# Attention and two MoE layers on one core: the first stretch's order rewritten by tile size of the matmuls, the last 64 keys of PV padded to 128 rows, and each buffer's turn stated

## Chip, core and metric

One core of a Trainium2 chip runs the whole program in one launch. The metric is device time in microseconds from the launch to its end, the median of the timed runs; lower is better. Engines are named as in the profile: PE (TensorE), DVE (VectorE), ACT (ScalarE), POOL (GpSimd), SP (SyncE, whose one queue issues every DMA here).

## What is computed

Attention with a memory term, a dense layer with gated product, and a layer of four experts, all in float32 (weights of the dense layer arrive as 64-bit floats). B=2, H=8, S=576, D=64; 1152 tokens of 512.

```python
scores = q @ k.T / sqrt(D)                      # causal mask, softmax
local = softmax(scores) @ v                     # "PV"
q_p = where(q > 0, q, exp(q) - 1) + 1           # phi
mem_out = (q_p @ M_prev) / (q_p @ z_prev + 1e-6)
x = g * mem_out + (1 - g) * local               # g = sigmoid(beta), per head
h = ((x @ w1) * (x @ w2)) @ w3; y = h @ w_out
out = sum_e p[:, e] * (relu(y @ e_w1[e]) @ e_w2[e])
```

## The kernel before

The program has three stretches. The first (to about 207 us) computes attention for eight pairs of heads, and on the way converts the dense layer's weights from 64-bit patterns, forms W = w3 @ w_out, and does the gated product of batch 0. The second does batch 0's product with W and batch 1's gated product; the third is the four experts. Only the first is touched.

The first stretch's work is cut into parts of a few instructions, each a Python function under a short name, and `FIRST` (line 20) is a hand-stated list of these names: the parts are recorded in its order, and each engine, and SP's DMA queue, runs its own instructions in that order. An instruction waits until its inputs are there and its output buffer is free, and everything behind it on its engine waits with it.

A query row of 576 is four blocks of 128 (each head apart) and 64 more rows, which the two heads of a pair share as halves of one tile. For pair p the parts are:

- `@qp`, `@kp`, `@Vp`: loads of q, k, and both heads' v (SP).
- `sp0` to `sp3`: scores (PE; L253, tile 64x128, for query blocks 0 and 1, then 2, then 3; L242, 128x128, for the last 64 rows). `mpk`: mask and row minimum (DVE, L269). `xpk`: exponential (ACT, L274).
- `tpg`: transposes of the probabilities in seven groups (PE, L307); `cpg`: their copy to SBUF (ACT, L311). Group 6 is the last 64 keys of the last query block: 64 columns are transposed, giving a 64x128 tile.
- `vp0`, `vp1`: PV of each head (PE, L330), the output in halves of 64 columns, tile 128x64. `vp2`: PV of the last 64 rows (L340), four key blocks of 128 rows in tile 128x64 and the last of 64 rows in tile 64x64.
- `ep`, `fp`: phi (ACT, DVE). `np`: memory term (PE, L364 at 128x128, and for the last 64 rows two matmuls into column halves, L368, 128x64: a "column-half tail").
- `gp`, `jp`: normalising of memory term and PV out of PSUM (DVE, L350 to L356). `jap`: their sum (POOL). `zp`: transposes of the result (PE, L391) with their own column-half tail (L396). `zhp`, `zlp`: split of the result (ACT, DVE).

The dense layer's parts are `@o`, `@w`, `@b` (loads), `oa`/`od`/`oh`/`ol`, `wa`/`wd`/`wp`, `ba`/`bd`/`bp` (conversion: two ACT operations, two DVE operations L136 and L137, and splits), `w`u`_`k (PE, L473), `b`u`_`a (PE, L537), `y` (sums), `bs` (stores).

PSUM tiles of scores, memory term, PV and result share two buffers (tag S), transposes two (tag T), and the staged weights, converted floats and split weights have two or three each; a pool hands them out in turn. A staged weight load waits until its buffer's last user is done. float32 matmuls that are not in the r form run in two passes, so the profile counts two PE records for one such instruction of the program.

Of the kernel before, what the change touches and what calls it, by code (L numbers as in the profile page):

```python
# [19 lines left out]
@q0 @k0 @k1 @q1 e0 @V0 f0 s00 s01 @w0 m00 e1 m01 s02 x00 @V1 f1 s03 @o0 x01 m02 wa0 t00 @k2 t02 m03 @q2 s10 x02 wd0  # L20
@o1 s11 c00 wp0 c02 t01 m10 @o2 x03 t04 c01 s12 @w1 c04 m11 x10 t03 m12 v00 @mz c03 x11 t05 @bt v01 c05 x12 t06 t10
s13 c06 c10 e2 v02 m13 @q3 oa0 t14 gates j0 @k3 t13 c14 n0 @V2 x13 od0 t11 t12 s20 g0 c11 @o3 c12 oa1 m20 v10 ja0 c13
x20 t16 v11 f2 oh0 od1 t15 e3 s21 c15 ol0 @w2 c16 oa2 v12 m21 w0_0 oh1 j1 @V3 x21 s22 od2 s23 m22 t20 wa1 @w3 t22 m23
c20 n1 @k4 x22 wd1 @q4 s30 c22 g1 wp1 @w4 x23 t24 oh2 t21 m30 z0 c24 c21 ja1 t23 zh0 v20 c23 zl0 x30 f3 v21 oa3 ol1
# [24 lines left out]
""".split()
RING = 12  # L50
# [7 lines left out]
def kernel(  # L58
# [63 lines left out]
    def from64_acts(raw, tmp, nm):  # L122


        hi = raw[..., 1]
        shape = list(hi.shape)
        t = tmp.tile(shape, F32, tag="t64f", name=f"tf_{nm}", bufs=3)
# [58 lines left out]
    warm = psT.tile([P, 512], F32, tag="T", name="warm")  # L186
# [39 lines left out]
    def stage_a(p):  # L226
# [4 lines left out]
        def scores(*qb):  # L231
# [5 lines left out]
            ps = psS.tile([P, 2, 512], F32, tag="S", name=f"sc{qb[0]}_{p}")  # L237
# [22 lines left out]
        def peaks(qb, low=True, ex=True):  # L260
            for src, i, x in banks[qb]:
                w = src.shape[-1]
                if "mn" not in Pt:
                    Pt["mn"] = A2.tile([P, NS2 + 1], F32, tag="mn", name=f"mn{p}")
                one = Pt["mn"][:, 2 * i + x : 2 * i + x + 1]
                if (i, x) not in Pt:
                    Pt[i, x] = A2.tile([P, w], F32, tag=f"P{i}", name=f"P{i}_{2 * p + x}", bufs=3 if i < NB else 2)
# [25 lines left out]
    def stage_b(p):  # L293
# [5 lines left out]
        def trans(g):  # L299
            mine = GROUPS[g]  # L300
            kr = SB if mine[0][2] == NB else P

            def f():
                st[g] = ps = psT.tile([P, 512], F32, tag="T", name=f"pt{g}_{p}")[0:kr, 0 : P * len(mine)]
                for y, (i, x, j) in enumerate(mine):
                    k0 = j * P if i < NB else 0 if j == NB else SB + j * P
                    nc.tensor.transpose(ps[:, y * P : (y + 1) * P], prob_t[p][i, x][:, k0 : k0 + kr], identF)  # L307

            def copy():
                t = A1.tile([kr, P * len(mine)], F32, tag=f"pt{g}", name=f"pT{g}_{p}")  # L310
                nc.scalar.copy(t, st.pop(g))  # L311
                for y, n in enumerate(mine):
                    pt[n] = t[:, y * P : (y + 1) * P]

            parts.update({f"t{p}{g}": f, f"c{p}{g}": copy})

        def slots(nm):
            ps = psS.tile([P, 2, 512], F32, tag="S", name=f"{nm}{p}")
# [64 lines left out]
        def fin():  # L383
# [3 lines left out]
            st["x"] = ps = psS.tile([P, 1024], F32, tag="S", name=f"x{p}")[:, 0:S]  # L387
# [13 lines left out]
        def fin_lo():  # L401
# [4 lines left out]
            f"n{p}": mem, f"g{p}": mem_out, f"v{p}0": pv(0), f"v{p}1": pv(1), f"v{p}2": pv_last, f"j{p}": join,  # L406
            f"ja{p}": join_mem, f"z{p}": fin, f"zh{p}": fin_hi, f"zl{p}": fin_lo,
# [11 lines left out]
    def staging(nm):  # L419

        stage_n[0] += 1
        if stage_n[0] > RING:
            return pf.tile([P, 4, P, 2], U32, tag="raw", name=nm)
# [28 lines left out]
    def w_conv(u):  # L452
# [8 lines left out]
        def split():  # L461
            w3s[u] = pf.tile([P, 2, 4, P], F32R, tag="ws", name=f"w3s{u}")
# [38 lines left out]
    class BUnits:  # L501
# [23 lines left out]
        def conv(self, u):  # L525
            f = self.raw.pop(u)
            self.ws[u] = ws = self.pool.tile([P, 2, KD, P], F32R, tag="ws", name=f"ws{self.b}_{u}")
# [310 lines left out]
    def b1_prods(m):  # L838
# [20 lines left out]
        def keep(i):  # L859
            def f():  # L860
                if i == 0:
                    st["u"] = pf.tile([P, 3, HS], F32, tag="ws", name=f"u{m}")
# [301 lines left out]
```

## Time and profile before

| | |
|---|---|
| median of 3 timed runs | 687.31 us (687.28 to 687.6) |
| span of the profiled execution, first to last instruction | 685.4 us |
| what the median has beyond that span | 1.9 us |
| PE, DVE, ACT, POOL busy in the span | 99%, 65%, 56%, 54% |

The profile times each instruction of each engine. A PE record's end is modelled, and matmuls overlap, so the cost of a block of matmuls is read from its start to the start of what follows it. The two numbers ahead of a PE form, as in 128*64, are the rows and columns of the array that it uses, the tile size.

### The profile page before, as it was taken

The page shows a single profiled execution, that of the slowest core. Times are in us where ns is not written, and L with a number is a line of the kernel's source. Part 1 is how long each engine was busy: PE and PEld are TensorE (multiplying, and loading weights), DVE is VectorE, ACT ScalarE, POOL GpSimd, SP SyncE. Part 2 cuts the span into 40 slices and gives each one's busy share as a digit, 9 for nine tenths or more (in the row PEclk, how much of TensorE's full clock was granted, in tenths as well). Part 3 has the DMA queues.
Part 4 walks back from the last instruction along what each step waited for, and adds up shares of the span by engine and source line. Part 5 has one row for each costly group of instructions (what it writes and reads, how often), then busy time and mean ns, then how long its engine had stood idle before and what let it go on. Part 6 is the DMA issues. An engine that isn't in the chain of part 4 may idle for free.

```text
span 685.4 us, 12814 instructions
## 1 busy us (share of the span) xinstructions
PE 675.7 (99%) x4877; PEld 605.1 (88%) x4877; DVE 447.5 (65%) x839; ACT 382.5 (56%) x808; POOL 368.6 (54%) x366
## 2 busy tenths in 40 slices
PE   8999999999999999999999999999999999999997
PEld 5778799888999999998989998889999899989896
DVE  6689788998858499458575644356553556543563
ACT  6897787576744366454545554455544455553541
POOL 2034645565542111617777765677766678656660
PEclk9999999999999999999999999999999999999999
DMA  9556266633631212113213231323231132313401
GB/s 286 176 169 219 71 198 192 174 109 124 185 139 34 90 62 94 55 35 98 62 62 123 77 109 62 112 73 107 79 121 64 62 124 64 122 61 109 154 32 62
DMA packets 43405, 74.53 MB, mean 109 GB/s; under 512 B 14416, under 2 KB 14416, under 8 KB 43344
## 3 DMA queue, kind: packets, MB, share of 16 engines
q1 hardware_dynamic: 43344, 73.72, 33.9%
q8 instruction: 38, 0.62, 0.4%
q14 instruction: 23, 0.19, 0.1%
HBM read 67.15 MB, written 6.55 MB: 108 GB/s over the span
## 4 chain that ended last, share of the span: by engine, by line
PE 88%; DVE 6%; ACT 3%; issue 1%; DMA 1%; SPq 0%; DVEq 0%; ACTq 0%
PE o L990 28%; PE Z L1037 14%; PE c L587 7%; PE Q L1037 7%; PE wacc L473 7%; PE ab L537 5%; PE Zb L853 4%; PE R L1037 3%; PE a L330 2%; PE pt L307 2%; PE Qb L853 2%; PE sc L253 2%; ACT P L274 1%; DVE P L269 1%; PE Rb L853 1%
## 5 line engine op out<-in xcount | busy, mean ns | idle before, releaser
L990 PE MATMUL o<-w,he 128*128 128x512 f32 x864 | 224.8, 393 | 0.0
L104 POOL TENSOR_TENSOR w<-r,w 128x512 fp32r<-128x512 f32 x96 | 130.6, 1361 | 120.3 <-ACT w L728 120.2
L990 PEld LDWEIGHTS o<-w,he 128*128 128x128 f32 x864 | 153.8, 188 | 24.1
L975 ACT ACTIVATE he<-t 128x320 fp32r<-128x320 f32 (+1 forms) x96 | 42.7, 445 | 120.6 <-DVE t L1066 73.3
L976 DVE SCALAR_TENSOR_TENSOR he<-t,he 128x320 fp32r<-128x320 f32 (+1 forms) x96 | 57.4, 598 | 49.1 <-ACT he L975 49.1
L1059 DVE TENSOR_TENSOR t<-u,Q 128x320 f32<-128x320 f32 (+1 forms) x32 | 14.6, 455 | 83.2 <-ACT u L1057 83.2
L107 DVE TENSOR_TENSOR w<-r,w 128x512 fp32r<-128x512 f32 x64 | 66.2, 1036 | 0.0
L728 ACT CAST w<-r 128x512 fp32r<-128x512 f32 x96 | 58.9, 614 | 0.0
L537 PE MATMUL ab<-xT,ws 128*128 128x288 f32 x384 | 55.4, 299 | 1.2 <-ACT asb L547 0.7
L537 PEld LDWEIGHTS ab<-xT,ws 128*128 128x128 f32 x384 | 51.5, 188 | 3.1 <-issue 1.3
L587 PE MATMUL c<-hT,W 128*128 128x288 f32 (+2 forms) x384 | 52.6, 295 | 0.0
L587 PEld LDWEIGHTS c<-hT,W 128*128 128x128 f32 x384 | 51.6, 188 | 0.0
L1037 PE MATMUL Z<-X0T,w 128*128 128x320 f32 x288 | 50.2, 310 | 0.2 <-ACT s L1047 0.2
L1037 PEld LDWEIGHTS Z<-X0T,w 128*128 128x128 f32 x288 | 46.0, 188 | 4.4 <-ACT s L1047 0.6
L473 PE MATMUL wacc<-wo,w3s 128*128 128x512 f32 x192 | 48.2, 400 | 0.0
L1037 PEld LDWEIGHTS Z<-X1T,w 128*128 128x128 f32 x288 | 40.8, 189 | 4.1
L473 PEld LDWEIGHTS wacc<-wo,w3s 128*128 128x128 f32 x192 | 35.0, 188 | 8.8 <-issue 1.0
L1037 PE MATMUL Z<-X1T,w 128*128 128x256 f32 x288 | 42.1, 282 | 0.0
L269 DVE CUSTOM_DVE_ANT_0 P<-sc,mask 128x128 f32<-128x128 f32 (+4 forms) x72 | 33.7, 516 | 11.4 <-PE sc L253 6.4
L758 ACT CAST w<-r 128x512 fp32r<-128x512 f32 x64 | 39.5, 619 | 0.0
L274 ACT ACTIVATE P<-P,mn 128x128 f32<-128x128 f32 (+4 forms) x72 | 37.7, 582 | 1.0 <-DVE mn L269 0.9
L101 POOL TENSOR_SCALAR w3s<-tf_l 128x512 fp32r<-128x512 f32 x16 | 12.8, 799 | 43.9 <-DVE tf_l L137 33.3
(170 smaller groups left out, 1322.1 us busy)
## 6 DMA issues: line engine op xcount, KB each, us to landing
r<-in_moe_w_dram SPq DMA_DIRECT2D x64, 256.0 KB, 3.0
r<-in_moe_w_tiles_dram SPq DMA_DIRECT2D x64, 256.0 KB, 3.7
w3r<-in_moe_w_tiles_dram SPq DMA_DIRECT2D x16, 512.0 KB, 3.6
wr<-in_moe_w_tiles_dram SPq DMA_DIRECT2D x16, 512.0 KB, 4.0
wor<-in_moe_w_out_dram SPq DMA_DIRECT2D x8, 512.0 KB, 4.4
wf<-tf SPq DMA_DIRECT2D x16, 256.0 KB, 4.2
wr<-wf SPq DMA_DIRECT2D x16, 256.0 KB, 2.9
qd<-in_q_cols_dram SPq DMA_DIRECT2D x8, 352.0 KB, 4.3
```

Of the source, the lines that this page charges most:

```text
L104: nc.gpsimd.tensor_sub(dst, src, r32(hi))
L107: nc.vector.tensor_sub(dst, src, r32(hi))
L274: nc.scalar.activation(Pt[i, x], Pt[i, x], AF.Exp, bias=one, scale=-1.0)
L473: nc.tensor.matmul(wacc[u], lhsT=w3s[u][:, a, c, :], rhs=wo[4 * g + c][:, bb, :], start=(c == 0 and x == 0), stop=(c == 3 and x == 2),)
L537: nc.tensor.matmul(ps[:, 0:HS], lhsT=self.ws[u][:, wi, kk, :], rhs=xT[b, kk][:, xi, a * HS : (a + 1) * HS], start=(n == 0), stop=(n == 3 * ...
L587: nc.tensor.matmul(st["ps"], lhsT=Wt[kk][:, wi, d * P : (d + 1) * P], rhs=hT[kk][:, xi, t0 : t0 + tw], start=(kk == 0 and x == 0), stop=(k ...
L728: return lambda: nc.scalar.copy(st["w"][i][:, 0], src(i))
L853: nc.tensor.matmul(st[d], lhsT=b1_set[m][a][:, wi, kk, :], rhs=BX[b][:, xi, kk, :], start=first and kk == 0 and x == 0, stop=(kk == 1 and ...
L975: nc.scalar.activation(h[:, 0], src, AF.Relu)
L976: nc.vector.scalar_tensor_tensor(out=h[:, 1], in0=src, scalar=0.0, in1=r32(h[:, 0]), op0=ALU.max, op1=ALU.subtract)
L990: nc.tensor.matmul(o_ps[i], lhsT=h_of[s][x][:, a, i * P : (i + 1) * P], rhs=w2s[s][x][:, b, :], start=first, stop=last,)
L1037: nc.tensor.matmul(ps, lhsT=w1s[s][a][:, wi, kk, :], rhs=X[c, b][:, xi, kk, :], start=first and kk == 0 and x == 0, stop=(kk == 1 and x == ...
```

## The change

1. `vp2` uses 128 rows for the last 64 keys: group 6 is transposed in full (the other 64 columns hold other keys' probabilities), its copy is 128x128, and rows 64 to 127 of the values' last block are zero, the column of ones included (four small memsets on POOL at the start).
2. The column-half tails of `np` and `zp` become parts of their own, `ntp` and `ztp`, which `FIRST` places apart from them.
3. `FIRST` is rewritten up to the product with W. The number of matmuls is the same.
4. A table `TURNS` says for ten tags which buffer each tile takes, in the order of the requests, in place of the pool's own turns.

```diff
-@q0 @k0 @k1 @q1 e0 @V0 f0 s00 s01 @w0 m00 e1 m01 s02 x00 @V1 f1 s03 @o0 x01 m02 wa0 t00 @k2 t02 m03 @q2 s10 x02 wd0
+@k0 @q0 @k1 @q1 @o0 @w0 @mz s00 e0 s02 m00 x00 m02 s01 x02 m01 s03 x01 f0 t00 @k2 s10 c00 @o1 m03 wa0 @V1 m10 t04 t03
...
+TURNS = {
+    "T": "010110010101010101010010101000100101001010101110100111101",
+    "S": "01010101010100110101011010100101001001001010101010001110",
...
+    def turn(pool, shape, dtype, tag, bufs, name):
+
+        n = used[tag] = used.get(tag, -1) + 1
+        own = TURNS.get(tag, "")
+        return pool.tile(shape, dtype, tag=f"{tag}{own[n] if n < len(own) else n % bufs}", name=name, bufs=1)
...
         nc.gpsimd.memset(t[:, :, D : D + 1], 1.0)
+        nc.gpsimd.memset(t[SB:P, NB, D : D + 1], 0.0)
...
-            kr = SB if mine[0][2] == NB else P
...
-                st[g] = ps = psT.tile([P, 512], F32, tag="T", name=f"pt{g}_{p}")[0:kr, 0 : P * len(mine)]
+                st[g] = ps = turn(psT, [P, 512], F32, "T", 2, f"pt{g}_{p}")[:, 0 : P * len(mine)]
...
-                    nc.tensor.transpose(ps[:, y * P : (y + 1) * P], prob_t[p][i, x][:, k0 : k0 + kr], identF)
+                    nc.tensor.transpose(ps[:, y * P : (y + 1) * P], prob_t[p][i, x][:, k0 : k0 + P], identF)
...
-                        st["a"][0][o, NB], lhsT=pt[NB, 0, j][:, o], rhs=v4[(2 * p + x) % 4][0:kr, j, :],
+                        st["a"][0][o, NB], lhsT=pt[NB, 0, j][:, o], rhs=v4[(2 * p + x) % 4][:, j, :],
...
+
+        def mem_last():
             for x in range(2):
                 nc.tensor.matmul(
-                    m[0][x * SB : (x + 1) * SB, NB], lhsT=phi_t[p][:, NB * P : S], rhs=mz[:, p, x], start=True, stop=True
+                    st["n"][0][x * SB : (x + 1) * SB, NB], lhsT=phi_t[p][:, NB * P : S], rhs=mz[:, p, x], start=True, stop=True
                 )
...
-            for x in range(2):
-                o = slice(x * SB, (x + 1) * SB)
-                nc.tensor.matmul(ps[o, NB * P :], lhsT=st["q"][:, NB], rhs=identF[:, o], start=True, stop=True)
+
+        def fin_last():
+            for x, o in enumerate(halves):
+                nc.tensor.matmul(st["x"][o, NB * P :], lhsT=st["q"][:, NB], rhs=identF[:, o], start=True, stop=True)
```

How the order moves, at three places. First PE around the PV of pair 1, before (`a` is PV's output, `v` the values, `pT` the copied transposes, `pt` the transposes, `P` probabilities, `sc` scores; L330 is `v10` and `v11`, L340 begins `v12`):

```order
L253 MATMUL sc_2_433<-kd_216,qd_225 128x256 x2
L330 MATMUL a_464<-v_106,pT_1_364 64x65 x8
L330 MATMUL a_464<-v_106,pT_1_445 64x65 x8
L330 MATMUL a_464<-v_106,pT_1_409 64x65 x4
L307 MATMUL pt_1_492<-identF,P_2_378 64x128
L330 MATMUL a_464<-v_107,pT_1_449 64x65 x8
L330 MATMUL a_464<-v_107,pT_1_486 64x65 x8
L330 MATMUL a_464<-v_107,pT_1_409 64x65 x4
L307 MATMUL pt_1_520<-identF,P_2_378 128x128 x4
L253 MATMUL sc_2_527<-kd_216,qd_225 128x384 x2
L340 MATMUL a_464<-v_106,pT_1_530 64x65
```

and in the changed kernel (L327 are the transposes, L383 the memory term, L350 and L359 PV):

```order
L383 MATMUL b_493<-mz,phi_326 128x130 x4
L327 MATMUL pt_1_500<-identF,P_2_315 128x128 x4
L327 MATMUL pt_1_509<-identF,P_2_315 128x128
L350 MATMUL a_511<-v_106,pT_1_454 64x65 x8
L350 MATMUL a_511<-v_106,pT_1_468 64x65 x8
L350 MATMUL a_511<-v_106,pT_1_491 64x65 x4
L350 MATMUL a_511<-v_107,pT_1_422 64x65 x8
L350 MATMUL a_511<-v_107,pT_1_498 64x65 x8
L350 MATMUL a_511<-v_107,pT_1_491 64x65 x4
L359 MATMUL a_511<-v_106,pT_1_563 64x65
```

The transposes of the last query block now stand ahead of all of the pair's PV, whose three parts follow each other; the two matmuls of the memory term's tail come right behind them.

Second, PE at the start, before:

```order
L253 MATMUL sc_0_159<-kd_146,qd_144 128x256 x2
L253 MATMUL sc_0_164<-kd_146,qd_144 128x384 x2
L253 MATMUL sc_0_184<-kd_146,qd_144 128x512 x2
L242 MATMUL sc_0_196<-kd_146,qd_144 128x288 x2
L307 MATMUL pt_0_211<-identF,P_0_170 128x128
```

and in the changed kernel:

```order
L274 MATMUL sc_0_161<-kd_148,qd_150 128x256 x2
L274 MATMUL sc_0_168<-kd_148,qd_150 128x512 x2
L274 MATMUL sc_0_188<-kd_148,qd_150 128x384 x2
L263 MATMUL sc_0_197<-kd_148,qd_150 128x288 x2
L327 MATMUL pt_0_205<-identF,P_0_172 128x128
```

The scores of block 3 (512 keys) stand ahead of those of block 2 (384); the first transposes use block 2.

Third, SP's queue behind the first loads, before (`kd`, `qd` are k and q, `wor` a staged weight of w_out, `w3r` of w3, `v` values):

```order
L430 DMA wor_199<-in_moe_w_out_dram 128x1024
L779 DMA pr<-in_probs_rows_dram 128x36
L180 DMA kd_216<-in_k_cols_dram 128x576
L180 DMA qd_225<-in_q_cols_dram 128x704
L430 DMA wor_236<-in_moe_w_out_dram 128x1024
```

and in the changed kernel:

```order
L452 DMA wor_258<-in_moe_w_out_dram 128x1024
L205 DMA v_104<-in_v_rows_dram 128x5x64
L205 DMA v_105<-in_v_rows_dram 128x5x64
L452 DMA wor_317<-in_moe_w_out_dram 128x1024
L201 DMA qd_324<-in_q_cols_dram 128x704
L472 DMA w3r_352<-in_moe_w_tiles_dram 128x1024
```

Pair 2's q, which stood ahead of the second staged w_out tile (o1), stands behind the fourth (o3, `wor_317`); pair 0's values come as the fifteenth and sixteenth load instead of the fifth and sixth.

## Rows read from the trace of the kernel before

**Rows 1.** Page, part 1: busy us, share of the span, instructions.
```profile
PE 675.7 (99%) x4877; PEld 605.1 (88%) x4877; DVE 447.5 (65%) x839; ACT 382.5 (56%) x808; POOL 368.6 (54%) x366
```
**Rows 2.** Busy time by stretch: stretch, length, PE, PEld, DVE, ACT, POOL, PEclk, DMA, GB/s.
```profile
0.00:206.90 206.90, 201.23 (x1950) 168.84 (x1951) 167.80 (x380) 150.12 (x292) 95.92 (x97) 1.00 0.55 169
```
**Rows 3.** Waits of PE in the first stretch: us in total, times, longest.
```profile
PE pt L307 <- ACT pT L311: 1.1, 2, 0.7
PE ab L537 <- ACT asb L547: 0.7, 1, 0.7
PE sc L253 <- DVE mn L269: 0.5, 2, 0.3
PE ab L537 <- DVE asb L551: 0.5, 1, 0.5
PE sc L242 <- DVE xm L356: 0.4, 1, 0.4
```
**Rows 4.** Timeline of PE, 90 to 98 us: start us, length us, line, form.
```profile
90.50 0.34 PE L368 MATMUL b<-mz,phi 128*64 128x65 f32 x4
90.76 1.09 PE L307 MATMUL pt<-identF,P 128*128 128x128 f32 x8
91.78 0.96 PE L253 MATMUL sc<-ks,qs 64*128 64x128 f32 x12
92.67 0.66 PE L307 MATMUL pt<-identF,P 128*128 128x128 f32 x4
93.26 1.39 PE L330 MATMUL a<-v,pT 128*64 128x65 f32 x40
94.58 3.44 PE L537 MATMUL ab<-xT,ws 128*128 128x288 f32 x24
97.85 0.60 PE L307 MATMUL pt<-identF,P 128*128 128x128 f32 x4
```
**Rows 5.** Timeline of PE, 41 to 47 us.
```profile
41.19 2.55 PE L330 MATMUL a<-v,pT 128*64 128x65 f32 x80
43.67 0.77 PE L307 MATMUL pt<-identF,P 128*128 128x128 f32 x5
...
46.11 0.95 PE L340 MATMUL a<-v,pT 128*64 128x65 f32 x20
46.99 0.97 PE L473 MATMUL wacc<-wo,w3s 128*128 128x512 f32 x3
```
**Rows 6.** Groups by line and form: copies of the transposes; busy us, mean ns, idle before.
```profile
L311 ACT COPY pT<-pt 128x512 f32<-128x512 f32 x48 | 27.1, 587 | 7.3 <-PE pt L307 7.0
L311 ACT COPY pT<-pt 64x128 f32<-64x128 f32 x8 | 2.1, 259 | 1.0 <-PE pt L307 1.0
```
**Rows 7.** Timeline of POOL: its first operation behind the set-up, idle time in brackets.
```profile
13.50 0.62 POOL L101 TENSOR_SCALAR w3s<-tf_l 128x512 fp32r<-128x512 f32 x1 [10.64 <-DVE tf_l L137]
```
**Rows 8.** Timeline of PE: first transposes, and first scores of pair 2.
```profile
10.16 1.04 PE L307 MATMUL pt<-identF,P 128*128 128x128 f32 x8
...
25.98 0.93 PE L253 MATMUL sc<-kd,qd 64*128 64x128 f32 x8
```
**Rows 9.** Timeline of DVE: m02, m03, the end of m12, od0's second operation.
```profile
10.01 0.68 DVE L269 CUSTOM_DVE_ANT_0 P<-sc,mask 128x512 f32<-128x512 f32 x1
...
11.23 0.76 DVE L269 CUSTOM_DVE_ANT_0 P<-sc,mask 128x576 f32<-128x576 f32 x1
...
16.29 0.69 DVE L269 CUSTOM_DVE_ANT_0 P<-sc,mask 128x512 f32<-128x512 f32 x1
...
25.01 0.69 DVE L137 SCALAR_TENSOR_TENSOR tf_wo<-wor,tf_wo 128x512 uint32<-128x512 uint32 x1
```
**Rows 10.** SP's issue of q2; loads of q to 60 us, KB, median us to landing.
```profile
10.79 0.37 SPq L180 DMA_DIRECT2D qd<-in_q_cols_dram  x1
qd<-in_q_cols_dram SPq DMA_DIRECT2D x7, 352.0 KB, 4.3
```
**Rows 11.** Busy time in the densest twenty us of DVE, columns as in rows 2.
```profile
120.00:140.00 20.00, 20.00 (x211) 17.09 (x210) 19.00 (x44) 12.15 (x25) 12.71 (x12) 1.00 0.60 175
```

More of the change, by code (lines that the diff above doesn't have):

```diff
@@ L19 @@
 FIRST = """
-@q0 @k0 @k1 @q1 e0 @V0 f0 s00 s01 @w0 m00 e1 m01 s02 x00 @V1 f1 s03 @o0 x01 m02 wa0 t00 @k2 t02 m03 @q2 s10 x02 wd0
[L21 to L24, printed above, removed]
@@ new lines @@
+e1 @bt wd0 s12 c03 @o2 s11 x03 @V0 m12 c04 wp0 oa0 t01 m11 t06 s13 c06 x11 od0 t02 n0 c01 oa1 m13 @o3 t05 @q2 f1 nt0
+v00 @w2 c02 @k3 gates c05 od1 v01 x10 g0 v02 oh1 oh0 t12 @V2 t10 ol0 c12 s20 j0 x12 @w1 t11 m20 c10 ja0 s22 oa2 ol1
+s21 c11 x13 m21 t14 e2 t13 m22 c14 n1 c13 t15 od2 x21 t16 v10 wa1 f2 @w3 v11 @q3 c15 wd1 c16 x22 v12 nt1 wp1 x20 w0_0
+j1 t21 w0_1 g1 c21 s23 oa3 t24 ja1 e3 @q4 m23 z0 @k4 oh2 od3 zt0 c24 s30 wa2 w1_0 ol2 @w4 t23 zh0 f3 w1_1 oh3 c23 t20
+zl0 w0_2 m30 c20 t22 x23 w1_2 wd2 hq4 t26 e4 s32 wa3 s31 ol3 @w7 @b4 m32 c26 c22 w1_3 wd3 w0_3 y1 n2 wa4 m31 @o6 wp3
@@ new lines @@
+oa6 lk5 y7 od6 t44 bp1 s50 ba2 b0_1 m50 f5 t42 bc00 oh6 s52 bc01 ol6 s51 c42 bd2 c44 b1_0 x43 ba3 m51 @b5 bp2 bs2 t41
+b1_1 c41 bd3 x50 t45 s53 ba4 rm00 @o7 bp3 m52 b2_0 @k6 c45 bs3 rh00 rm01 bd4 rh01 t46 b2_1 ba5 rl01 rl00 n5 bd5 bc20
+bc21 b3_0 bp4 x52 m53 @b7 oa7 t54 bs5 b3_1 c46 od7 x53 t43 rm10 @b6 bp5 nt5 rm11 v40 rh10 c43 rh11 hk6 v41 rl11 hq6
+lk6 x51 v42 b4_0 j4 c54 lq6 e6 ba6 rl10 b4_1 g5 ja4 oh7 bc40 t50 bc41 s60 c50 bd6 b5_0 ba7 ol7 bs6 @w8 bp6 t51 rm20
+@q7 b5_1 m60 rh20 c51 rl20 s62 rm21 bd7 s61 rh21 x60 b6_0 m62 @w9 bp7 wa8 bs7 t52 x62 s63 wd8 b6_1 rl21 @w10 f6 bc60
@@ new lines @@
+rl60 v72 b14_0 j7 ja6 g7 b14_1 bc140 ja7 b15_0 bc141 b15_1 rm70 rh70 z6 rm71 z7 rl70 zt7 zt6 k00_0 zh6 zl6 rh71 k00_1
+zh7 zl7 rl71 k00_2 k00_3 k01_0 kc00 k01_1 k01_2 k01_3 k10_0 kc01 k10_1 k10_2 k10_3 k11_0 kc10 k11_1 k11_2 k11_3 k20_0
+kc11 k20_1 k20_2 k20_3 k21_0 kc20 k21_1 k21_2 k21_3 k30_0 kc21 k30_1 k30_2 k30_3 kc30 k31_0 k31_1 k31_2 k31_3 kc31
+""".split()
+TURNS = {
+    "T": "010110010101010101010010101000100101001010101110100111101",
+    "S": "01010101010100110101011010100101001001001010101010001110",
+    "P0": "0120102101201201",
+    "P1": "0120102101201201",
+    "P2": "0120120121021021",
+    "P3": "0121021021021021",
+    "P4": "01010101",
+    "t64f": "0120121020102120210210101010120120102010",
+    "ws": "01101010101010101010101010101010010101010",
+    "raw": "0101010110100101010010101010101010101",
+}
@@ L126, in from64_acts @@
         shape = list(hi.shape)
-        t = tmp.tile(shape, F32, tag="t64f", name=f"tf_{nm}", bufs=3)
+        t = turn(tmp, shape, F32, "t64f", 3, f"tf_{nm}")
         u = tmp.tile(shape, U32, tag="t64u", name=f"tu_{nm}", bufs=1)
@@ L184, in load_head @@
         nc.sync.dma_start(out=v4[n % 4][:, :, 0:D], in_=v[n])
-    warm = psT.tile([P, 512], F32, tag="T", name="warm")
+    warm = turn(psT, [P, 512], F32, "T", 2, "warm")
     for _ in range(13):
@@ L236, in scores @@
             last = len(passes) - 1
-            ps = psS.tile([P, 2, 512], F32, tag="S", name=f"sc{qb[0]}_{p}")
+            ps = turn(psS, [P, 2, 512], F32, "S", 2, f"sc{qb[0]}_{p}")
             if qb[0] == NB:
@@ L266, in peaks @@
                 if (i, x) not in Pt:
-                    Pt[i, x] = A2.tile([P, w], F32, tag=f"P{i}", name=f"P{i}_{2 * p + x}", bufs=3 if i < NB else 2)
+                    Pt[i, x] = turn(A2, [P, w], F32, f"P{i}", 3 if i < NB else 2, f"P{i}_{2 * p + x}")
                 if low:
@@ L300, in trans @@
             mine = GROUPS[g]
-            kr = SB if mine[0][2] == NB else P
             def f():
-                st[g] = ps = psT.tile([P, 512], F32, tag="T", name=f"pt{g}_{p}")[0:kr, 0 : P * len(mine)]
+                st[g] = ps = turn(psT, [P, 512], F32, "T", 2, f"pt{g}_{p}")[:, 0 : P * len(mine)]
                 for y, (i, x, j) in enumerate(mine):
                     k0 = j * P if i < NB else 0 if j == NB else SB + j * P
-                    nc.tensor.transpose(ps[:, y * P : (y + 1) * P], prob_t[p][i, x][:, k0 : k0 + kr], identF)
+                    nc.tensor.transpose(ps[:, y * P : (y + 1) * P], prob_t[p][i, x][:, k0 : k0 + P], identF)
             def copy():
-                t = A1.tile([kr, P * len(mine)], F32, tag=f"pt{g}", name=f"pT{g}_{p}")
+                t = A1.tile([P, P * len(mine)], F32, tag=f"pt{g}", name=f"pT{g}_{p}")
                 nc.scalar.copy(t, st.pop(g))
@@ L317, in slots @@
         def slots(nm):
-            ps = psS.tile([P, 2, 512], F32, tag="S", name=f"{nm}{p}")
+            ps = turn(psS, [P, 2, 512], F32, "S", 2, f"{nm}{p}")
             return [ps[:, g, 0 : n * (D + 1)].rearrange("p (s d) -> p s d", d=D + 1) for g, n in ((0, NB + 1), (1, NB))]
@@ L385, in fin @@
                 xf.append(main.tile([P, 2, S], F32, tag=f"g{H // 2 + len(xf)}", name=f"xf{len(xf)}"))
-            st["x"] = ps = psS.tile([P, 1024], F32, tag="S", name=f"x{p}")[:, 0:S]
+            st["x"] = ps = turn(psS, [P, 1024], F32, "S", 2, f"x{p}")[:, 0:S]
             for i in range(NB):
@@ L405, in stage_b @@
         parts.update({
-            f"n{p}": mem, f"g{p}": mem_out, f"v{p}0": pv(0), f"v{p}1": pv(1), f"v{p}2": pv_last, f"j{p}": join,
-            f"ja{p}": join_mem, f"z{p}": fin, f"zh{p}": fin_hi, f"zl{p}": fin_lo,
+            f"n{p}": mem, f"nt{p}": mem_last, f"g{p}": mem_out, f"v{p}0": pv(0), f"v{p}1": pv(1), f"v{p}2": pv_last, f"j{p}": join,
+            f"ja{p}": join_mem, f"z{p}": fin, f"zt{p}": fin_last, f"zh{p}": fin_hi, f"zl{p}": fin_lo,
         })
@@ L422, in staging @@
         if stage_n[0] > RING:
-            return pf.tile([P, 4, P, 2], U32, tag="raw", name=nm)
+            return turn(pf, [P, 4, P, 2], U32, "raw", 2, nm)
         return main.tile([P, 4, P, 2], U32, tag=f"g{H // 2 + stage_n[0] % 4}", name=nm)
@@ L461, in split @@
         def split():
-            w3s[u] = pf.tile([P, 2, 4, P], F32R, tag="ws", name=f"w3s{u}")
+            w3s[u] = turn(pf, [P, 2, 4, P], F32R, "ws", 2, f"w3s{u}")
             hi_pool(w3s[u][:, 0], st["f"])
@@ L526, in conv @@
             f = self.raw.pop(u)
-            self.ws[u] = ws = self.pool.tile([P, 2, KD, P], F32R, tag="ws", name=f"ws{self.b}_{u}")
+            self.ws[u] = ws = turn(self.pool, [P, 2, KD, P], F32R, "ws", 2, f"ws{self.b}_{u}")
             self.hi(ws[:, 0], f)
@@ L861, in f @@
                 if i == 0:
-                    st["u"] = pf.tile([P, 3, HS], F32, tag="ws", name=f"u{m}")
+                    st["u"] = turn(pf, [P, 3, HS], F32, "ws", 2, f"u{m}")
                 nc.scalar.copy(st["u"][:, i], st["Z"])
@@ L868, in f @@
                 if i == 0:
-                    st["t"] = pf.tile([P, 3, HS], F32, tag="raw", name=f"t{m}")
+                    st["t"] = turn(pf, [P, 3, HS], F32, "raw", 2, f"t{m}")
                 nc.vector.tensor_add(st["t"][:, i], st["u"][:, k], st[d])
```

41 lines of the change are left out of this document (16 added, 25 removed).

## The prediction, made before the changed kernel ran

> **What bounds the kernel now.** First the page's busy shares: PE is busy for 675.7 of 685.4 us, and no other engine passes 65% [rows 1]. Then busy time by stretch: in the first stretch, which the change replans (0 to 206.9 us), PE is busy for 201.2 us, DVE for 167.8, ACT for 150.1, POOL for 95.9, at a granted clock of 1.00 [rows 2]. Then the waits of PE: after the warm-up transposes it waited five kinds of time in the first stretch, 1.1 + 0.7 + 0.5 + 0.5 + 0.4 = 3.2 us in all [rows 3]. So the end is set by what PE itself needs, not by what it waits for.
>
> "Busy" hides a loss, which the timeline shows: from a row's start to the next row's start is what a block of equal matmuls costs. Eight transposes between two blocks of another tile size cost 91.78 - 90.76 = 1.02 us, four cost 93.26 - 92.67 = 0.59, so one more costs 0.108 and the block itself 0.16 [rows 4]. Forty PV records cost 94.58 - 93.26 = 1.32 [rows 4], eighty cost 43.67 - 41.19 = 2.48 [rows 5]: 0.029 a record, 0.16 a block. The four records of a column-half tail (L368) cost 90.76 - 90.50 = 0.26 where four more in a block cost 0.12: 0.14 for the block [rows 4]. The last query block's PV (L340, 16 records of tile 128x64 and then 4 of 64x64) costs 46.99 - 46.11 = 0.88 where twenty records cost 0.58: 0.30, two blocks of 0.15 [rows 5]. Each change of tile size costs about 0.155 us, whichever way it goes.
>
> **The change part by part.** Counted in the order of PE's instructions, by the tile size of each matmul, the kernel changes tile size 111 times, the changed one 54 times: entries into 128x64 fall from 37 to 13, into 64x64 from 8 to 0, into 64x128 (scores) from 19 to 15, and returns to 128x128 from 47 to 26. That is 24 + 8 + 4 + 21 = 57 fewer, with the same number of matmuls. All of it lies on PE, which sets the end: 57 x 0.155 = **8.8 us off**. The scores' four are priced like the rest, with no row of their own; at nothing they would take 0.6 off the sum.
>
> Is 0.155 all returned? At a boundary the next block starts 0.07 before the row's modelled end (0.66 long, next start after 0.59), while a block of 24 L537 matmuls that is followed by its own tile size is overlapped by 0.17 (3.44 long, next start 97.85 - 94.58 = 3.27 later) [rows 4]. So 0.10 of the 0.155 is overlap lost at the boundary; the rest I put down to a second weight load that comes late after it. I take both as saved, because a block of 80 shows neither in its middle [rows 5]. [...]
>
> Padding: the eight 64-column transposes become ordinary 128-column ones (0.108 us each, what they cost now when they stand among transposes); the 64x128 ACT copies, now 0.259 us [rows 6], still have 128 elements a partition. At worst each becomes as long as a 512-element copy (0.59), 8 x 0.33 = 2.6 us, under ACT's 57 us of idle time; nothing on the path. Four more memsets stand on POOL, which does nothing until 13.50 [rows 7]: nothing.
>
> The start is replanned too. DVE now runs m00, m02 and m01 before the first transposes t00 can have their input, where m00 and m01 were enough. So the transposes that began at 10.16 [rows 8] come behind one more mask step, 11.23 - 10.01 = 1.22 us on DVE [rows 9]; the two exponentials that belong to it run on ACT beside the next mask step. Bounds: nothing, because two phi steps leave that chain, to 1.2 us; I take **0.5 us lost**, nearer to nothing since PE has the next pair's scores and transposes to do, and because the values (V0) are needed later than now.
>
> On SP, the load of q2 now stands behind o3, and o3 waits for the join of o0 (od0) on DVE, because it takes over that buffer. Before, q2 was issued at 10.79, and such a load lands 4.3 us after its issue [rows 10]. DVE had all that now stands ahead of od0 done by 16.98 [rows 9]; with its two operations of 0.69 each the join ends near 18.4 instead of 25.70 [rows 9], q2 lands near 23. Pair 2's scores began at 25.98 [rows 8], and in the new order they have three transposes (1.3) and a wait of 0.7 less ahead: about 24.0. Margin 1 us, cost nothing; without that margin each us of delay is paid in full.
>
> The waits of 3.2 us: the new order leaves more PE work between a bank's release and its next use (s22 had one weight product between itself and the PV whose bank it takes; now it has three sets of transposes and a score block). But DVE is denser once PE is faster. I take them as unchanged, with bounds of -3.2 (all gone) and +4.4 (below). The stated buffers add no instruction; they only name which buffer each tile takes.
>
> Sum: 685.4 - 8.8 + 0.5 = 677.1 us of span. The span is 1.9 us short of the median of the timed runs, 687.31, for what lies around it. **Forecast 679.0 us.**
>
> **The rivals.**
> - *DVE and ACT cannot feed a faster PE.* Between 120 and 140 us DVE was busy for 19.00 of 20 us [rows 11]; with PE 4.3% faster (8.8 of 206.9) that is 99%. For it: the masks, joins and splits are the same number. Against: over the whole stretch DVE has 39 us to spare, and PE's order keeps weight products as filler. If half the gain turns into waits: 679.0 + 4.4 = 683.4.
> - *Only the lost overlap comes back*, 57 x 0.10 = 5.7, and the late second weight load is paid inside the longer blocks: 685.4 - 5.7 + 0.5 + 1.9 = 682.1. For it: no row shows a tail and a long PV block joined. Against: the 80-record block. [...]
> - *The waits go as well*: 679.0 - 3.2 = 675.8.
> - *Slower: SP's queue at q2.* If od0 ends late, o3 holds q2, w2, k3 and V2 behind it, s20 waits, and PE's in-order queue has everything of pair 2 behind s20. At od0's old end of 25.70, q2 lands near 30.3 and PE loses 6 us: 685. It decides from od0 ending at about 29, where 10 us are lost: 689. For it: the margin is 1 us. Against: od0's exponent copies stand early in ACT's order, and o0 is now the fifth load instead of the tenth.
> - *No effect*: if the price hung on the kind of matmul rather than on the boundary, only the start changes: 687.8.
>
> **How the numbers follow.** A measurement of this kernel can tell about 0.2% (1.4 us) from no change. Chances: forecast 0.60, feed 0.15, overlap alone 0.10, waits gone 0.05, no effect 0.05, slower 0.05. The first four are all faster by over 0.2% (below 685.9): 0.90; same 0.05; slower 0.05. The range takes the four: 675.5 to 684.0.
>
> **What would show it.** Right: PE waits of 2 to 4 us in the first stretch; the product with W (L609 in the changed kernel) beginning some 8 us before 206.9; PV blocks of 96 to 100 records with the tails in them, at 0.16 of overhead a block; nothing changed after it. Feed rival: PE waits for DVE mn or ACT pT of 5 us and more. Overlap rival: the first pairs inside joined blocks stay slow. Slower: one long wait of PE at the scores of pair 2, ended by a landing of qd. Wrong altogether: 54 boundaries in the trace and the stretch no shorter.

## Result, and the profile after

The changed kernel takes 678.66 us (median of 4 runs, 678.51 to 679.87) against 687.36 for the kernel before on the same chip: ratio 0.9875, 95% interval 0.9861 to 0.9889. On another chip, run again, it took 678.75 (678.36 to 679.14). The forecast was 679.0 us, 675.5 to 684.0.

Busy time by engine, page, part 1 (before: [rows 1]):

```profile
PE 666.8 (99%) x4877; PEld 602.4 (89%) x4877; DVE 438.0 (65%) x839; ACT 382.0 (56%) x808; POOL 370.2 (55%) x370
```

PE ran the same 4877 records in 8.9 us less. Where it gained is seen from the first matmul of the product with W, the end of the replanned stretch; the line of that product, before and then after:

```profile
L587 PE MATMUL c<-hT,W x384: 278/294/314, 206.8 to 307.8; 128*128 128x288 f32 x96, 128*128 128x320 f32 x48, 128*128 128x256 f32 x48
```

```profile
L609 PE MATMUL c<-hT,W x384: 278/295/401, 197.7 to 299.0; 128*128 128x288 f32 x96, 128*128 128x320 f32 x48, 128*128 128x256 f32 x48
```

It begins 9.1 us earlier. What follows it takes 479.0 us (676.7 - 197.7), before 478.6 (685.4 - 206.8): nothing changed there but 0.4 us the other way. Busy time in the first stretch after, columns as in [rows 2]:

```profile
0.00:198.20 198.20, 192.45 (x1953) 166.20 (x1954) 157.20 (x381) 148.03 (x290) 95.03 (x98) 1.00 0.55 171
```

PE's waits in the first stretch after (before: [rows 3], 3.2 us):

```profile
PE sc L274 <- DVE mn L290: 1.2, 2, 0.6
PE sc L263 <- DVE mn L290: 1.1, 3, 0.4
PE pt L327 <- ACT pT L331: 0.7, 1, 0.7
PE a L350 <- DMA v<-in_v_rows_dram: 0.5, 1, 0.5
```

3.5 us in all: as much as before, at other places. So the gain is not waiting; it is time in which PE counted as busy. PV of pair 1, timeline of PE after:

```profile
28.98 2.56 PE L350 MATMUL a<-v,pT 128*64 128x65 f32 x80
31.41 0.80 PE L359 MATMUL a<-v,pT 128*64 128x65 f32 x20
32.04 0.28 PE L389 MATMUL b<-mz,phi 128*64 128x65 f32 x4
32.26 0.97 PE L495 MATMUL wacc<-wo,w3s 128*128 128x512 f32 x3
```

From start to start the 104 records take 3.28 us; the same three pieces standing apart took 2.48 + 0.88 [rows 5] + 0.26 [rows 4] = 3.62. This is one of the first three such blocks, which cost 3.28 to 3.50 us; why they cost more than the others is open. The other five, from 66 us on, cost 3.18 or 3.19, for example (106.76 - 103.58):

```profile
103.58 0.34 PE L389 MATMUL b<-mz,phi 128*64 128x65 f32 x4
103.74 2.51 PE L350 MATMUL a<-v,pT 128*64 128x65 f32 x80
106.08 0.76 PE L359 MATMUL a<-v,pT 128*64 128x65 f32 x20
106.76 1.45 PE L559 MATMUL ab<-xT,ws 128*128 128x288 f32 x9
```

That is 104 x 0.029 = 3.02 us and 0.16 for the block: one price where four were paid (0.16, twice 0.15, 0.14). The same sum over the whole first stretch, by kind of matmul (from each record's start to the next one's, all idle time of PE taken out): transposes 25.6 us before, 21.8 after; PV 27.8 and 24.3; the tails 4.1 and 3.5; scores 29.0 and 27.5. The W products went the other way, 46.3 and 47.7: they now fill gaps in 32 runs, before in 16. The transposes gained as much as PV, since they too are entered less often from another tile size: 22 times before, 5 times after.

### The profile page after: what moved, and what is told of

Read it like the earlier page. It is cut to its first block, busy times and chain, and to the rows that moved or that the text cites. A ratio compares the mean times of both kernels' runs of the same rounds, so it can differ in the third digit from the quotient of the medians.

```text
span 676.7 us, 12796 instructions
## 1 busy us (share of the span) xinstructions
PE 666.8 (99%) x4877; PEld 602.4 (89%) x4877; DVE 438.0 (65%) x839; ACT 382.0 (56%) x808; POOL 370.2 (55%) x370
## 4 chain that ended last, share of the span: by engine, by line
PE 59%; DVE 2%; ACT 1%; issue 0%
PE o L1012 28%; PE Z L1059 14%; PE Q L1059 7%; PE c L609 4%; PE R L1059 4%; PE Zb L875 1%; PE Qb L875 1%; DVE w L127 0%; DVE x L696 0%; DVE he L998 0%; ACT he L997 0%; DVE X1B L127 0%; DVE prs L803 0%; ACT w L750 0%; DVE t L1088 0%
## 5 line engine op out<-in xcount | busy, mean ns | idle before, releaser
L495 PE MATMUL wacc<-wo,w3s 128*128 128x512 f32 x192 | 52.2, 408 | 0.0
L495 PEld LDWEIGHTS wacc<-wo,w3s 128*128 128x128 f32 x192 | 33.6, 189 | 7.9 <-issue 0.8
```

The source lines that it names most:

```text
L495: nc.tensor.matmul(wacc[u], lhsT=w3s[u][:, a, c, :], rhs=wo[4 * g + c][:, bb, :], start=(c == 0 and x == 0), stop=(c == 3 and x == 2),)
```

## The experiments

All times are medians; "the changed kernel" is 678.7 us in each comparison.

**The parts of the change.** First, PV cut up again: two products stand in between PV's three parts, in seven pairs (`w`, in pairs 4 and 7 `b`; 28 changes of tile size more, 82 in all):

```diff
-... v10 wa1 f2 @w3 v11 @q3 c15 wd1 c16 x22 v12 nt1 wp1 x20 w0_0 j1 t21 w0_1 g1 ...
+... v10 wa1 f2 @w3 w0_0 v11 @q3 c15 wd1 c16 x22 w0_1 v12 nt1 wp1 x20 j1 t21 g1 ...
```

> The changed kernel with one weight product moved in between the parts of PV of each of seven pairs, nothing else: 82 changes of tile size instead of 54, the same instructions. My theory (a change of tile size costs 0.155 us of PE, paid in full): 28 x 0.155 = 4.3 us more than the changed kernel, about 683.0, and PE's waits unchanged within 1 us. Rival, only the lost overlap is paid (0.10): 2.8 us more, about 681.5. Rival, the boundary costs nothing and the gain came from the new order's dependencies: 678.7, within 0.7.

Measured: 692.49 us (ratio to before 1.0068, 1.0055 to 1.008), 13.8 more than the changed kernel, three times what 28 boundaries should cost. Its PE waits, the larger ones:

```profile
PE sc L264 <- DVE mn L291: 2.3, 4, 0.9
PE sc L275 <- DVE mn L291: 1.4, 4, 0.6
PE sc L264 <- DVE rm L370: 1.3, 2, 0.8
PE sc L275 <- DVE xq L376: 1.3, 2, 0.9
```

With the smaller ones they come to 10.0 us. Two readings were possible: a PV that is drawn out holds its PSUM bank longer, or the moved weight products are missed at the places they left. The control moves the same products, for six pairs, in one piece ahead of an uncut PV:

```diff
-... t16 v10 wa1 f2 @w3 v11 @q3 c15 wd1 c16 x22 v12 nt1 wp1 x20 w0_0 j1 t21 w0_1 g1 ...
+... t16 w0_0 w0_1 v10 wa1 f2 @w3 v11 @q3 c15 wd1 c16 x22 v12 nt1 wp1 x20 j1 t21 g1 ...
```

> A control for the split PV (692.5 us): the same twelve weight products of six pairs leave their places, but stand in one piece ahead of the pair's PV (and of the tail in front of it), so PV stays whole and the count of changes is 54 as in the changed kernel (pair 7's two products stay). If the 13.8 us of the split were, beyond 28 changes x 0.155 = 4.3 us, the price of a PV whose parts stand apart (its PSUM bank and the join come later), this comes out near the changed kernel: 678 to 681. If they were the price of taking fillers from where PE needed them, it comes out at 685 to 690, with waits at the scores as in the split.

Measured: 689.74 us (1.0035, 1.0023 to 1.0046), with 54 changes like the changed kernel. Its waits:

```profile
PE wacc L495 <- DVE both L509: 2.3, 3, 1.2
PE sc L263 <- DVE mn L290: 2.3, 4, 0.9
...
PE sc L263 <- DVE rm L369: 1.3, 2, 0.8
PE sc L274 <- DVE xq L375: 1.3, 2, 0.9
```

The waits for `rm` and `xq` are the same, to the tenth, with PV cut and with PV whole. So the bank theory falls, and 11 of the 13.8 us come with the products' places. Only a part of these 11 is the cover that was meant: the waits of all scores rose from 2.3 us to 6.1 (6.3 with PV cut), because scores that take over the bank of a memory term or of PV need a product in front of them, in which DVE empties that bank. Another 4.3 us in the control are waits of products themselves, for their own bank or their weights, and of the 9.9 us by which its profiled first stretch exceeds that of the changed kernel 2.6 stand in no wait. Between the two kernels, cut and whole, lie 28 changes (and the place of pair 7's two products): 2.75 us of medians plus the control's 0.8 us more of waits make 0.13 each, and the intervals of the two medians leave 0.04 either way. By the first stretches of the two profiled runs, which end at 212.1 and 207.6, less 0.6 by which the first transposes began later (10.22 and 9.59), it is (4.5 - 0.6 + 0.8) / 28 = 0.17.

The column-half tails put back behind their memory terms and transposes (74 changes):

```diff
-... t02 n0 c01 oa1 m13 @o3 t05 @q2 f1 nt0 ...
+... t02 n0 nt0 c01 oa1 m13 @o3 t05 @q2 f1 ...
```

> The changed kernel with the two column-half tails attached again to the memory term and to the result's transposes: 74 changes of tile size instead of 54. My theory: 20 x 0.155 = 3.1 us more than the changed kernel, about 681.8. Rival, overlap alone: 2.0 more, 680.7. Rival, a tail needs its own block only where something waits for it, so nothing is paid: 678.7.

Measured: 680.2 us (0.9898, 0.9884 to 0.9911), 1.5 more where 3.1 were forecast. A tail among others costs in this trace what it cost before:

```profile
29.33 0.34 PE L389 MATMUL b<-mz,phi 128*64 128x65 f32 x4
29.59 0.76 PE L327 MATMUL pt<-identF,P 128*128 128x128 f32 x5
```

0.26 us for four records, as in [rows 4]. Its profiled execution is the slowest of the four (682.27). There the first stretch is 3.65 us longer than the changed kernel's: 0.8 is the start (10.40 and 9.59), 0.5 are waits behind it (3.15 us against 2.65), and 2.3 are left for twenty changes, 0.12 each. Why that is less than 0.155 isn't settled, and the interval of the median is 0.9 us either way.

The padding undone, and the padding alone on the kernel before:

```diff
-                st[g] = ps = turn(psT, [P, 512], F32, "T", 2, f"pt{g}_{p}")[:, 0 : P * len(mine)]
+                st[g] = ps = turn(psT, [P, 512], F32, "T", 2, f"pt{g}_{p}")[0:kr, 0 : P * len(mine)]
...
-                        st["a"][0][o, NB], lhsT=pt[NB, 0, j][:, o], rhs=v4[(2 * p + x) % 4][:, j, :],
+                        st["a"][0][o, NB], lhsT=pt[NB, 0, j][:, o], rhs=v4[(2 * p + x) % 4][0:kr, j, :],
```

> The changed kernel with the padding undone: the last 64 keys are again transposed from 64 columns and multiplied with 64 rows. By tile size alone the boundaries go from 54 to 77, and 23 x 0.155 = 3.6 us more, about 682.2. If a 64-column transpose among full ones counts as no boundary (it cost 0.108 there before), only the eight blocks of tile 64x64 come back: 8 x 0.15 = 1.2 more, about 679.9. Rival, padding is worth nothing by itself: 678.7.

Measured: 679.26 us (0.9876, 0.986 to 0.9891), 0.6 more than the changed kernel.

```diff
+        nc.gpsimd.memset(t[SB:P, NB, D : D + 1], 0.0)
...
-            kr = SB if mine[0][2] == NB else P
+            kr = P
```

> The kernel before with the padding alone, order and tails as before: 105 changes of tile size instead of 111 when all 64-column transposes are counted as 128x64, and eight fewer blocks of 64x64. My theory: 0.9 to 1.5 us less than before, 685.9 to 686.5. Rival, nothing: 687.4. Rival, the wider copies on ACT delay transposes behind them in the ACT-bound start: up to 1 us more, 688.4.

Measured: 686.71 us (0.9988, 0.9979 to 0.9997), 0.9 us off. Without padding the changed order has 77 changes by tile size; were each 0.155, undoing it would cost 3.6 us. It costs 0.6, with intervals that leave about 1.4 either way. The trace tells more: from start to start PV's last part (its line is L361 there) takes 6.71 us where the changed kernel's takes 5.35, 0.17 for each of eight blocks of 64x64, and the transposes take 21.8 in both. A 64-column transpose among full ones is a change by the count, but not by the time. From the padding alone (105 changes) to the changed kernel (54), the ratio to the kernel before falls from 0.9988 to 0.9875: 7.8 us for 51 changes, 0.15 each.

**The price of a change by itself.** The second stretch has 56 products of six r-form matmuls each, most of them one behind the other, with one wait of PE of 0.2 us. Ahead of each a float32 matmul was put, whose result is not used:

```diff
+                for i in range(1):
+                    nc.tensor.matmul(
+                        dum[0:64, i * SB : (i + 1) * SB], lhsT=r32(Wt[0][:, 0, 0:64]), rhs=r32(Wt[0][:, 0, 0:SB]), start=True, stop=True
+                    )
                 for kk in range(2):
```

> The changed kernel, with 56 float32 matmuls added whose result nobody reads, in the second stretch, one ahead of the six matmuls of each product of batch 1: 64 columns of weights, 64 columns of data, so tile 128x64 between blocks of tile 128x128; 112 more changes of tile size, at a place where PE waits for nothing. Each dummy's own two records cost what PV's do, 0.029 us each, 3.2 us in all. Theory (0.155 a change): 678.7 + 3.2 + 17.4 = 699.3. If only lost overlap is paid (0.10): 693. If a change costs nothing away from PV: 682. [...]

Measured: 703.34 us (1.0236, 1.0222 to 1.025). The same with 128 columns of weights (`dum[0:128, ...]`, `lhsT=...[:, 0, 0:128]`):

> The same 56 dummies at the same places, but with 128 columns of weights, so tile 128x128 like their neighbours and no change of tile size more than in the changed kernel. Theory: 678.7 + 3.2 = 681.9, up to 684 if a weight load of 128 columns is not hidden. If the price hangs on the kind of matmul (float32 in two passes among one-pass ones) and not on the tile size, it comes out as slow as the 64-column dummies (699).

Measured: 690.66 us (1.0043, 1.003 to 1.0055), 12 us over the changed kernel where 3 to 5 were expected: between the theory and its rival. Two of the 64-column ones in a row (`range(2)`):

> As the 64-column dummies, but two in a row at each place: 112 dummies, the same 112 more changes of tile size. Theory (the price is paid per change): the 64-column dose plus 56 x 0.058 = 3.2 us, so 702.5. If every 64-column matmul pays by itself: twice the dose, near 720. If the pair hides part of the change under its second matmul: less than 3 us more.

Measured: 710.11 us (1.0329, 1.0315 to 1.0343). And the second of the two in the other column half of the array:

```diff
-                        dum[0:64, i * SB : (i + 1) * SB], lhsT=r32(Wt[0][:, 0, 0:64]), ...
+                        dum[i * SB : (i + 1) * SB, 0:SB], lhsT=r32(Wt[0][:, 0, 0:64]), ...
```

> As the pairs of 64-column dummies (710.1 us), but the second of each pair goes to the other column half (array columns 64 to 127), as PV's matmuls do by turns; the same 112 dummies and the same 112 more changes of tile size. A dummy behind another in the same half cost 0.12 us there, where PV's two records cost 0.058. If halves by turns run beside each other as in PV, the pair costs what one dummy did, within 0.03 either way: 703.3 to 706.6. If the 0.12 has another cause (the operands, or float32 behind one-pass matmuls), the time stays at 710.

Measured: 703.34 us (1.0233, 1.0219 to 1.0247), the time of a single dummy. Timelines of PE at one and the same place; without dummies (the changed kernel) a product takes 0.80 us from start to start, the mean of ten:

```profile
238.34 0.96 PE L875 MATMUL Zb<-BXB,b1w 128*128 128x288 f32 x6
239.15 0.96 PE L875 MATMUL Zb<-BXT,b1w 128*128 128x288 f32 x6
```

One dummy of 64 columns:

```profile
240.99 0.33 PE L876 MATMUL dum<-W 128*64 128x64 f32 x2
241.25 1.06 PE L881 MATMUL Rb<-BXB,b1w 128*128 128x288 f32 x6
242.24 0.33 PE L876 MATMUL dum<-W 128*64 128x64 f32 x2
```

One of 128 columns:

```profile
240.18 0.33 PE L876 MATMUL dum<-W 128*128 128x64 f32 x2
240.31 1.03 PE L881 MATMUL Zb<-BXT,b1w 128*128 128x288 f32 x6
241.19 0.33 PE L876 MATMUL dum<-W 128*128 128x64 f32 x2
```

Two of 64 columns in one half:

```profile
241.24 0.45 PE L876 MATMUL dum<-W 128*64 128x64 f32 x4
241.62 1.06 PE L881 MATMUL Zb<-BXT,b1w 128*128 128x288 f32 x6
242.61 0.45 PE L876 MATMUL dum<-W 128*64 128x64 f32 x4
```

Two of 64 columns in the two halves:

```profile
241.10 0.34 PE L876 MATMUL dum<-W 128*64 128x64 f32 x4
241.37 1.06 PE L881 MATMUL Rb<-BXB,b1w 128*128 128x288 f32 x6
242.36 0.34 PE L876 MATMUL dum<-W 128*64 128x64 f32 x4
```

The periods are 0.80, 1.25, 1.01, 1.37 and 1.26 us. A second dummy in the same half costs 0.12, in the other half 0.01: halves run beside each other. That is why PV, whose matmuls take the halves by turns, shows 0.029 a record; a lone dummy has no partner and itself lasts 0.12 (an estimate: what the second one in the same half added), not the 0.058 that the first three expectations took. So 1.25 - 0.80 - 0.12 = 0.33 us are left for a dummy's two changes, **0.165 each**; by the medians, (703.34 - 678.75 - 56 x 0.12) / 112 = 0.16. The forecast's 0.155 holds where nothing waits, and "only lost overlap" (0.10) and "costs nothing away from PV" fall. The 128-column dummy splits the price: the two kernels differ by 12.7 us, 0.113 for each of 112 changes, so about 0.11 goes with the tile size, and some 0.05 of the 0.16 is paid by a short float32 matmul among long r-form ones without any change of tile size (an estimate: (1.01 - 0.80 - 0.11) / 2, with 0.11 for the two records of the dummy, which begin 0.055 us apart). What that 0.05 is was not tried.

**The waits that are left.** Five of the names in front of PE's waits were moved (the expectation counts six), PE's own order kept:

```diff
-... @o0 @w0 @mz s00 ... e1 @bt wd0 s12 c03 @o2 s11 x03 @V0 m12 c04 ...
+... @o0 @w0 @V0 @mz s00 ... e1 @bt s12 c03 @o2 s11 x03 m12 wd0 c04 ...
...
-... t30 wa7 w5_0 wp4 @b0 w5_1 zh1 e5 zl1 w5_2 c30 wd7 ... s42 y4 od5 ... w6_1 m42 @b3 ...
+... t30 c30 wa7 w5_0 wp4 @b0 w5_1 zh1 e5 zl1 w5_2 wd7 ... s42 m42 y4 od5 ... w6_1 @b3 ...
...
-... yh10 wd13 w12_0 ... y11 m70 t62 ...
+... yh10 m70 wd13 w12_0 ... y11 t62 ...
```

> The changed kernel with six names of the order moved: the load of the first values ahead of the memory matrices' load, wd0 behind m12, c30 ahead of wa7, m42 right behind s42, m70 ahead of wd13. PE's own order stays, with its 54 changes of tile size. It aims at five of the waits that PE still has in the first stretch (0.5 for the values, 0.4 at s13, 0.7 at t35, 0.4 at s43, 0.6 at s71; 2.6 us in all). If waits are repaid by what is moved behind (od5, wd13 and wa7 later): 678 to 679. If they are plain: 676.1 to 677.5. Rival: one of the delayed conversions makes a weight product late, and nothing is gained or up to 1 us is lost.

Measured: 683.64 us (0.9939, 0.9927 to 0.9952), 5.0 more than the changed kernel; the rival, and larger than it was thought. Its larger waits:

```profile
PE b L383 <- DVE mn L290: 2.3, 1, 2.3
PE sc L274 <- DMA qd<-in_q_cols_dram: 1.1, 1, 1.1
PE b L383 <- DVE xT L127: 1.0, 1, 1.0
PE a L350 <- DVE mn L290: 1.0, 2, 0.8
```

The longest lasts from 81.0 to 83.3 us, where the memory term of pair 4 needs a bank that m41 frees. DVE there, with m42 moved ahead:

```profile
76.78 0.69 DVE L290 CUSTOM_DVE_ANT_0 P<-sc,mask 128x512 f32<-128x512 f32 x1 [0.54 <-PE sc L274]
...
78.00 1.85 DVE L156 SCALAR_TENSOR_TENSOR tf_wo<-tf_wo,tu_wo 128x512 uint32<-128x512 uint32 x1
79.89 0.69 DVE L157 SCALAR_TENSOR_TENSOR tf_wo<-wor,tf_wo 128x512 uint32<-128x512 uint32 x1
81.27 1.00 DVE L127 TENSOR_TENSOR wo<-tf_wo,wo 128x512 fp32r<-128x512 f32 x1 [0.69 <-ACT wo L464]
82.19 0.54 DVE L290 CUSTOM_DVE_ANT_0 P<-sc,mask 128x384 f32<-128x384 f32 x1
```

m42 now waits 0.54 for its scores, and od5 and its split, pushed behind it, hold m41 up (82.19; 77.33 in the changed kernel). c30 and m42 took their own waits away too (against the changed kernel the lag fell by 0.9 us at 64 us and by 0.7 at 77), but 1.3 us had come in at 62 and 2.4 followed at 78. m70 alone left a gain: the lag fell by 0.9 us at 148 us, and 0.4 of that was gone again at 152. So m70 alone was kept, and the first values' load moved by one place:

```diff
-... s12 c03 @o2 s11 x03 @V0 m12 ...
+... s12 c03 @V0 @o2 s11 x03 m12 ...
...
-... yh10 wd13 w12_0 ... y11 m70 t62 ...
+... yh10 m70 wd13 w12_0 ... y11 t62 ...
```

> The changed kernel with two names moved, the two of the six moves that are left after the last run: the mask step m70 ahead of wd13 (there the lag of that run fell by 0.9 us at 148 us) and the first values' load ahead of o2's, one place up, not ahead of the memory matrices. Plain: 0.6 and 0.5 of wait go, 677.6 to 678.2. If the landing of V0 is set by what shares the DMA rings rather than by its place in the queue, only m70 counts: 678.1. Rival: o2's landing, later by one load, makes a conversion late, and it comes out at 679 or more.

Measured: 679.11 us (0.9876, 0.9861 to 0.9891), no gain. In its place stands one new wait:

```profile
24.46 0.93 PE L274 MATMUL sc<-kd,qd 64*128 64x128 f32 x8 [1.54 <-DMA qd<-in_q_cols_dram]
```

The values no longer come late, but q2, issued at 18.38 with the loads of o2 and o3 right in front of it, landed 5.9 us later; in the changed kernel, issued at 17.65, it took 3.8. The control for both:

> The changed kernel itself, once more, on the same chip as the two others, so that differences of a few tenths have a base: 678.7.

Measured: 678.75 us (0.9875, 0.9861 to 0.9888).

The stated buffers were not tried apart from the order: this order relies on them. No version here beats the changed kernel.

## Why the prediction was right, point by point

- **57 fewer changes, 8.8 us off.** Right in size, and in the cause, a price at each boundary. In the profiled executions the first stretch lost 9.1 us; 0.6 of it is the start (below), and PE's waits behind the start went from 2.9 to 2.6. That leaves 8.2 us for 57 boundaries, 0.145 each, against 0.155 from the rows of before and 0.16 in the dose. The scores' four changes, priced without a row, lie within that. The joined blocks show the price once, 0.16 or 0.17, in five of eight cases. The late second weight load, to which the prediction put a third of the price, shows in the trace before: in the PV block at 41.19 us the second pair of records has its weight loads 0.055 us behind the first pair's and begins 0.107 behind it, where inside the block one pair follows the other by 0.058. What was glossed over: "each change of tile size costs about 0.155" counts the padded transposes wrongly (0.6 us where the count gave 3.6 for the 23), and in the dose the price is not all the tile size's.
- **679.0 against 678.66.** That it is so close is in part luck: the boundaries gave 0.6 us less than forecast, and the 0.5 us lost at the start did not show in the time.
- **The padding costs nothing.** Right: alone it gained 0.9 us.
- **The start, 0.5 us lost.** Too much. The first transposes began at 9.59 us, before at 10.16 [rows 8], but that is no gain: it follows the length of PE's first scores, which differs from execution to execution (last section). In eleven profiled kernels with the changed kernel's start they began at 9.59 to 10.40, 10.02 on average; in the two with the start of before (it and the padding alone) at 10.16 and 9.69, 9.93 on average. Where the first scores were slow for equally long (the clock rose at 7.38 and 7.39 us), it is 10.16 with the start of before and 10.40 with that of the changed kernel: some 0.2 us lost, by one pair of executions. The step took DVE's chain for the bound.
- **"The values (V0) are needed later than now."** Missed: pair 0's PV waited 0.48 us for them. The clause looked at the scores and transposes in front, not at V0's own place in SP's queue, behind o2.
- **q2's margin.** Right. od0 ended at 17.2 (forecast 18.4), q2 was issued at 17.65 and landed at 21.5 (forecast 23), and pair 2's scores began at 22.82 without a wait. The run with V0 moved shows how thin this is.
- **Waits unchanged at 3.2.** They are 3.5: right. The rival "the waits go as well" was tried by hand, twice, and what was taken out came back elsewhere.
- **The feed rival (15%).** DVE did not fill up: 157.2 of 198.2 us, 79%, before 167.8 of 206.9, 81% [rows 2]. The forecast reckoned with the same DVE work in less time; the work itself became shorter (below).

## What to carry to other kernels

When PE is busy 99% of the time, look at the distance between the starts of neighbouring blocks, not at busy time: here most changes of tile size between blocks held about 0.15 us that no wait showed, and gathering the same matmuls into longer runs gave it back. Price such a reordering by boundaries, but keep the fillers where they cover a bank that another engine must empty: moving twelve of them cost 11 us, some 4 of them waits for such banks, and more in all than the boundaries were worth. Waits that are left in such an order pay for each other; take one out alone, and look for the next before believing the gain.

## What was not expected of the hardware

**DVE's conversions became shorter.** Groups by line of DVE, first stretch, before:

```profile
L136 DVE SCALAR_TENSOR_TENSOR tf_l<-tf_l,tu_l 128x512 uint32<-128x512 uint32 x16 | 17.0, 1061 | 0.4 <-ACT tf_l L130 0.4
...
L136 DVE SCALAR_TENSOR_TENSOR tf<-tf,tu 128x512 uint32<-128x512 uint32 x16 | 14.3, 892 | 2.7 <-ACT tf L130 2.7
```

and after:

```profile
L156 DVE SCALAR_TENSOR_TENSOR tf_l<-tf_l,tu_l 128x512 uint32<-128x512 uint32 x16 | 13.0, 814 | 4.2 <-ACT tf_l L150 4.2
L156 DVE SCALAR_TENSOR_TENSOR tf<-tf,tu 128x512 uint32<-128x512 uint32 x16 | 11.8, 736 | 5.5 <-ACT tf L150 5.3
```

The same 32 instructions took 31.3 us before and 24.8 after, and DVE's whole first stretch 10.6 us less. Only the first of a join's two operations gained: all 40 of L136 (128x512) took 39.1 us before and 30.7 after, all 40 of L137 32.8 and 33.0. In both traces 21 of the 40 first operations had no operation of POOL at the same time, and each of these took 0.68 to 0.69 us. The other 19 took 1.30 on average before, up to 2.10, and 0.86 after. So in both traces only operations with one of POOL's beside them were longer. The changed order has no fewer such meetings (19 of the 40 in both) and as much work on POOL (95.9 and 95.0 us); the meetings got shorter, 0.89 us each before and 0.45 after, on average. What makes such an operation longer was not tried.

**The first scores differ from execution to execution.** The first twelve score records, timeline of PE in the kernel before, and in the changed one:

```profile
4.95 2.74 PE L253 MATMUL sc<-kd,qd 64*128 64x128 f32 x12
```

```profile
4.94 1.78 PE L274 MATMUL sc<-kd,qd 64*128 64x128 f32 x12
```

In the repeat of the changed kernel they took 2.23 us, in the one with m70 and V0 moved 2.85. It goes with TensorE's granted clock. From start to start a pair of score records of 256 columns takes 426 ns in the kernel before (5.969 to 6.395 us) and 215 in the changed one (5.483 to 5.698). The trace's clock entries begin, at a granted clock of 1.00, at 7.38 us before and at 4.90 in the changed kernel (5.89 in the repeat, 7.14 with m70 and V0 moved). In the last three, which have the same order of scores, the later the entries begin, the longer the twelve records take, 1.78, 2.23 and 2.85 us. So by the spacing, 426 and 215 ns, the first scores of the kernel before ran at about half the changed kernel's speed; PE had run the warm-up transposes since 1.99 us, one every 213 ns. So the 1.00 of [rows 2] holds from 7.38 us on: ahead of it the trace has no entry, and a stretch without one is printed as 1.00. Over all the profiled kernels, first transposes at 9.59 to 9.77 us go with a rise at 4.90 to 5.53, 10.03 and 10.06 with one at 5.89 and 5.95, and 10.16 to 10.53 with one at 6.26 to 7.65. A profiled execution can so begin up to 1 us apart from another of the same order, which must not be read as the change's. Why the rise comes at another moment each time is open.

**Column halves run side by side.** A float32 matmul of 64 columns behind one in the other half of the array cost 0.01 us (the periods of 1.26 and 1.25 us above), behind one in the same half 0.12 (1.37 and 1.25).
